# Dilated and sliding-window attention with a GEGLU block: batch 1's dilated q, k turned by DMA, and values of late dilated pairs laid side by side again

## The chip, the cores and the metric

The kernel runs on one core of a Trainium2 chip. The metric is device time in microseconds, from several executions of each kernel; a smaller number is better. A profile of one execution comes with each kernel. TensorE is called PE in the profile, VectorE DVE, ScalarE ACT, GpSimd POOL and SyncE SP; a "q" behind a name means its queue, where transfers are issued.

## The reference

Attention runs over 8 batches of 8 heads, 576 tokens, 64 values a head. Heads 0 to 3 look back over a window of 32 tokens ("plain"), heads 4 to 7 over every fourth token of 128 ("dilated"). The result, 4608 rows of 512, goes through a gated layer of 1536 hidden values.

```python
mask_plain = (rel >= 0) & (rel < window)                                        # window 32
mask_dil = (rel >= 0) & (rel < window * dilation) & (rel % dilation == 0)       # dilation 4
scores = np.where(masks[None, :, :, :], scale * np.matmul(q, k.transpose(0, 1, 3, 2)), -1000000000.0)
attn = np.exp(scores - np.max(scores, axis=-1, keepdims=True))
attn = attn / (np.sum(attn, axis=-1, keepdims=True) + 1e-09)
x = np.matmul(attn, v)                       # then (batch, token) x (head, value) = 4608 x 512
# ...
g = x @ w_gate                               # 512 x 1536
gelu = 0.5 * g * (1.0 + erf(g * inv_sqrt2))
return (gelu * (x @ w_val) @ w_out).astype(np.float32)
```

## The kernel before

The work is ordered by hand; each engine runs its instructions in the order in which the program emits them. Heads are taken two at a time, so there are 32 "pairs": pairs 4b to 4b+3 belong to batch b. Two of each batch are plain and two dilated (in batches 2 and 3 the dilated ones come first). A pair has scores (`emit_s`: matmuls, then the exponential on ScalarE into a tile `P`, then the mask on VectorE), and values (`emit_pv` or `emit_both`: matmuls for the numerator and the denominator, then the division on VectorE into `xT`).

The gated layer is taken in 9 stages `c` of 512 tokens. A stage has a hidden layer (`ffn1`, 12 blocks of 8 matmuls; gelu on ScalarE, product on VectorE into `u_all`), then an output layer (`ffn2`, 4 blocks of 12 matmuls, one bank each). Scores and values of later pairs are set between these matmuls: `scores[c]` lists the pairs whose scores are made in stage c, `values_b[c]` those whose values are made in its output layer, `values_a[c]` those in its hidden layer (key: the block). `places` says after which matmul of which output block: v values, s scores, m mask, x division.

How batch 1 gets its turned dilated q and k (rows of eight tokens, 72 rows; 32 turns on TensorE through `ident`, then four copies out of PSUM):

```python
    def t_dil(b, hp, q8, b0, engs):
        qtd_ = tiles["qT", b][1]
        for t in range(2):
            for hl in range(2):
                for r in range(4):
                    c0 = ((hl * 2 + r % 2) * 2 + r // 2) * R8
                    nc.tensor.transpose(ps16[:, b0 + t, c0 : c0 + R8],
                        q8[:, t, 2 * hp + hl, 2 * r : 2 * r + 2, :].rearrange("p r d -> p (r d)"),
                        ident[0:R8, 0:R8])
            copy(engs[t], qtd_[...], ps16[...])          # cut

    # ... loads of batch 1
    sv1 = new_v(1)
    new_qt(1)
    qd1 = load_eights(1)
    wo1 = [load_wo(i) for i in range(3)][1]
    load_v_dil(1)
    q61 = ldp.tile([R6, 2, 6, HK, D], F16, tag="qp", name="qp1")
    for hp in range(2):
        for t in range(2):
            cast_six("pool", q61, st1, t, hp)
    gate["dma"] = wo1            # the next load on SyncE waits for this one to land
    v_plain(1, sv1, nc.sync)
    v_cast(1, sv1)
    tiles["plain", 2] = load_batch_plain(2)
```

Batches 2 to 7 are turned by DMA:

```python
    def load_batch_rest(b):
        # ...
        dst = qtd_.rearrange("p t h m i -> p (t h m) i")
        nc.sync.dma_start_transpose(out=dst[:, :, 0:P], in_=qd.rearrange("p t h r d -> p (t h r d)"))
        nc.sync.dma_start_transpose(out=dst[:, :, P:NCL], in_=rd.rearrange("p t h r d -> p (t h r d)"))
        # ...
        last_keys(b, 0, HK, nc.gpsimd)       # copies the last 64 keys of each class into kTr
```

Stage 0's output layer (pairs 4 and 5 are batch 1's plain ones, 6 and 7 its dilated ones; `third(tb, i)` is four output matmuls):

```python
            s_of(4)
            t_dil(1, 0, qd1, 0, ("dve", "dve"))
            t_dil(1, 1, qd1, 2, ("act", "dve"))
            mask_next()
            last_keys(1, 0, HK)
            third(0, 0)
            s_of(5)
            third(1, 0)
            mask_next()
            den(4, 0)
            s_of(6)
            third(0, 1)
            # ... cut
```

Values in the hidden layers, in one pass over v and ones: the tile of v holds v of one head, ones, v of the other head, so that 128 columns of it give a numerator and its denominator together. Dilated pairs do so in batches 5 to 7 only (`spread`):

```python
    def emit_both(n, b0):
        # ... plain pairs cut
                for s in range(2):
                    o = ps[:, b0 + 2 * hl + s, 0:DW].rearrange("p (m i) -> p m i", m=2)
                    src = pt[:, 2 * s + hl, :].rearrange("p (m i) -> p m i", m=2)
                    for m in range(2):
                        mm(o[:, m, 0:P], vd[:, hp, 2 * m + s], src[:, m, 0:P], hl, m == 0)
                    mm(o[:, :, P:NCL], vr[:, hp, s], src[:, :, P:NCL], hl, False)
```

Its division is two transposes of 64 rows (L537), a reciprocal, a transpose and two products of 64 rows (L550). `emit_pv` instead makes denominators by a matmul with ones and numerators by one with v, each for 64 output rows, and its division has one transpose (L576) and one product (L602) of 128 rows.

Of the kernel before, what the change touches and what calls it, by code (L numbers as in the profile page):

```python
# [9 lines left out]
F16 = mybir.dt.float16  # L10
# [11 lines left out]
def kernel(  # L22
# [14 lines left out]
    P = 128  # L37
# [22 lines left out]
    prb = ctx.enter_context(tc.tile_pool(name="prb", bufs=7))  # L60
# [17 lines left out]

# [4 lines left out]
            const.tile([P, HP, 4, 3, D], F16, tag=f"vd{i}", name=f"vd{i}"),  # L83
            const.tile([P, HP, 3, D], F16, tag=f"vt{i}", name=f"vt{i}"),
            const.tile([P, HP, 2, 3, D], F16, tag=f"vr{i}", name=f"vr{i}"),
# [65 lines left out]


    values_a = {3: {4: 16}, 4: {1: 20, 4: 21, 8: 22}, 5: {1: 24, 4: 25, 8: 26}, 6: {1: 28, 4: 29, 7: 30, 10: 31}}
    all_at = [n for at in values_a.values() for n in at.values()]
    spread = (5, 6, 7)

# [37 lines left out]
    def new_v(b):  # L194

        sv = ldp.tile([P, 5, HK, D], F32, tag="sv", name=f"sv{b}")
        tiles["v", b] = vset[b % 3]
        if b in spread and b - 3 not in spread:
            for t in vset[b % 3][1::2]:
                nc.gpsimd.memset(t.rearrange("p g r x d -> p (g r) x d")[:, :, 1, :], 1.0)  # L200
        return sv

    def side_by_side(t):

        n = HK * t.shape[2] * D
        flat = t.rearrange("p g r x d -> p (g r x d)")[:, 0:n]
        return flat.rearrange("p (h r d) -> p h r d", h=HK, d=D)

    def v_dil(b, h, s0, rest=False):

        t = tiles["v", b][3 if rest else 1]
        return t[:, h // 2, s0, 2 * (h % 2), :] if b in spread else side_by_side(t)[:, h, s0, :]
# [49 lines left out]
    def load_v(b, dst, src):  # L262

        if b not in spread:
            nc.gpsimd.dma_start(out=fl(side_by_side(dst)), in_=src)
            return
        for h in range(HK):
            nc.gpsimd.dma_start(  # L268
                out=dst[:, h // 2, :, 2 * (h % 2), :], in_=src[:, h, :].rearrange("p (r d) -> p r d", d=D)
            )  # L270

    def load_v_dil(b):
        load_v(b, tiles["v", b][1], quads(v, b, HK, 0, 4 * P))
        load_v_dil_rest(b)

    def load_v_dil_rest(b):
        for m in range(2):
            src = quads(v, b, HK, S - 256, S)[:, :, 2 * m * D : 2 * m * D + 2 * D]
            load_v(b, tiles["v", b][3][64 * m : 64 * m + 64], src)
# [11 lines left out]
    def load_batch_rest(b):  # L291
# [6 lines left out]
        qtp_, qtd_, _ = tiles["qT", b]  # L298
        dst = qtd_.rearrange("p t h m i -> p (t h m) i")
        nc.sync.dma_start_transpose(out=dst[:, :, 0:P], in_=qd.rearrange("p t h r d -> p (t h r d)"))  # L300
        nc.sync.dma_start_transpose(out=dst[:, :, P:NCL], in_=rd.rearrange("p t h r d -> p (t h r d)"))
        dst = qtp_.rearrange("p t h c -> p (t h) c")
# [14 lines left out]

    def in_one(n):

        return n in all_at and (is_plain(n) or n // NHP in spread)  # L320
# [108 lines left out]
    def emit_pv(n, b0, parts=("den", "num"), wide=False, flip=False):  # L429
# [4 lines left out]
        vp, _, vt, _ = tiles["v", b]  # L434
# [39 lines left out]
        else:  # L474
# [10 lines left out]
            if "num" in parts:  # L485
                for s in range(2):
                    for m in range(3):
                        for hl in range(2):
                            h, p0 = 2 * hp + hl, (2 * s + hl) * DW
                            if m < 2:  # L490
                                lhs, c0 = v_dil(b, h, 2 * m + s), 512 * (s + flip) + m * NCL
                                add(hl, c0, run(P), lhs, p0 + m * NCL, run(P), m == 0)
                            else:
                                two = [[NCL, 2], [1, 16]]
                                add(hl, 512 * (s + flip) + P, two, v_dil(b, h, s, True), p0 + P, two, False)
# [3 lines left out]
    def emit_both(n, b0):  # L499

        b, hp = n // NHP, n % 2
        pt = tiles["P", n]
        vp, vd, vt, vr = tiles["v", b]

        def mm(o, trio, rhs, hl, st):
            lhs = trio[:, hl : hl + 2, :].rearrange("p x d -> p (x d)")
            nc.tensor.matmul(o, lhs, rhs, start=st, stop=True, skip_group_check=True)  # L509

        for hl in range(2):
            if is_plain(n):
                for j in range(5):
                    w = (PW, PW, PW, P, PT)[j]
                    p0 = j * PW - (32 if j == 4 else 0)
                    o = ps[:, b0 + 2 * hl + j // 4, j % 4 * P : j % 4 * P + w]
                    mm(o, vp[:, j, hp] if j < 4 else vt[:, hp], pt[:, hl, p0 : p0 + w], hl, j in (0, 4))
            else:
                for s in range(2):
                    o = ps[:, b0 + 2 * hl + s, 0:DW].rearrange("p (m i) -> p m i", m=2)  # L520
                    src = pt[:, 2 * s + hl, :].rearrange("p (m i) -> p m i", m=2)
                    for m in range(2):
                        mm(o[:, m, 0:P], vd[:, hp, 2 * m + s], src[:, m, 0:P], hl, m == 0)
                    mm(o[:, :, P:NCL], vr[:, hp, s], src[:, :, P:NCL], hl, False)
# [4 lines left out]
    def norm_both_r(n, b0):  # L529
        dt = nrm.tile([P, 18, 32], F32, tag="dt", bufs=1)  # L530
        for hl in range(2):
            dst = dt[64 * hl : 64 * hl + 64].rearrange("p b c -> p (b c)")
            if is_plain(n):
                nc.vector.transpose(dst, both_rows(1 - hl, b0, hl))  # L534
            else:
                src = ps[64 - 64 * hl : 128 - 64 * hl, b0 + 2 * hl : b0 + 2 * hl + 2, 0:DW]
                nc.vector.transpose(dst.rearrange("p (s c) -> p s c", s=2), src)  # L537
# [440 lines left out]
```

The softmax here doesn't subtract the row's maximum and nothing guards it: scores larger than these inputs give would overflow.

## Time and profile before

| what | value |
|---|---|
| device time, median of 3 | 350.09 us (349.64 to 350.47) |
| span of the profiled run | 348.4 us |
| busy share PE / DVE / ACT / POOL | 97% / 60% / 43% / 29% |
| matmuls of the hidden layer (L627), 864 | 227.8 us busy |
| matmuls of the output layer (L661), 420 | 97.0 us busy |
| PE 20 to 43 us (hidden layer of stage 0), DMA | 211 GB/s |
| PE 43 to 62 us (output layer of stage 0) | 18.65 of 19.00 us busy |

In a line of the timeline the columns are start, duration, engine, line of the kernel, operation, tiles out<-in, shape and count; in brackets stands how long the engine was idle before, and what ended it. Busy times of PE overlap, as matmuls are pipelined, so the distance of starts tells more than their durations. In the list of waits the columns are total, count and longest wait. In the chain they are start, duration and what ran.

### The profile page before, as it was taken

To read this page: it belongs to the slowest core of one execution; us is meant where nothing else is said; L and a number is where in the kernel's file an instruction comes from. 1 tells how busy PE (TensorE), PEld (TensorE's weight loads), DVE (VectorE), ACT (ScalarE), POOL (GpSimd) and SP (SyncE) were. 2 spreads that over 40 slices of the span, in tenths; PEclk is the share of its full clock that TensorE was granted. 3 is DMA by queue.
4 is the path that set the end of the run, shared out by engine and by line. 5 is a ranking of instruction groups with operands and counts; after the bars stand their busy time and mean duration, and the time that the engine had idled before them with its cause. 6 is when DMAs were issued, how large, how long until landed. Compare 5 with 4: busy or idle time off the path is not lost.

```text
span 348.4 us, 6007 instructions
## 1 busy us (share of the span) xinstructions
PE 336.6 (97%) x2322; PEld 163.9 (47%) x2322; DVE 210.2 (60%) x317; ACT 148.1 (43%) x220; POOL 102.0 (29%) x154
## 2 busy tenths in 40 slices
PE   8979999999999999999999999999999999999996
PEld 3644454444544445444544444445444444444443
DVE  4884497533784379664989865996399723303320
ACT  2753372535543546336553456326532223323321
POOL 8693304630630560493009800670000000000000
PEclk9999999999999999999999999999999999999999
DMA  8999999999999999796169944991100020020002
GB/s 184 225 206 222 203 203 174 178 143 257 180 121 251 190 126 227 168 167 115 61 158 179 121 96 131 205 120 48 74 2 0 32 90 1 2 87 33 0 33 90
DMA packets 113037, 44.45 MB, mean 128 GB/s; under 512 B 91408, under 2 KB 108432, under 8 KB 113008
## 3 DMA queue, kind: packets, MB, share of 16 engines
q1 hardware_dynamic: 84192, 31.01, 38.4%
q0 software_dynamic: 28272, 12.33, 30.5%
q10 hardware_dynamic: 544, 0.72, 0.7%
q8 instruction: 18, 0.29, 0.3%
q14 instruction: 11, 0.09, 0.1%
HBM read 39.85 MB, written 9.44 MB: 141 GB/s over the span
## 4 chain that ended last, share of the span: by engine, by line
PE 71%; DVE 11%; DMA 10%; issue 3%; ACT 3%; SPq 1%; POOL 1%; DVEq 0%; POOLq 0%; ACTq 0%
PE ps L627 41%; PE ps L661 22%; DMA st<-in_k_dram 4%; PE ps L497 3%; DMA sv<-in_v_dram 3%; DMA wv<-in_moe_w_val_dram 3%; DVE u_all L650 2%; DVE dt L537 1%; DVE dt L576 1%; DVE xT L550 1%; PE ps L509 1%; PE ps L415 1%; DVE rb L587 1%; DVE P L425 1%; DVE xT L602 1%
## 5 line engine op out<-in xcount | busy, mean ns | idle before, releaser
L649 ACT ACTIVATE g<-ps 128x512 f16<-128x512 f32 x108 | 63.9, 597 | 124.4 <-PE ps L627 123.9
L650 DVE SCALAR_TENSOR_TENSOR u_all<-g,ps 128x512 f16<-128x512 f16 x108 | 72.5, 683 | 73.4 <-PE ps L627 63.1
L627 PE MATMUL ps<-xT,wv 128*128 128x512 f16 x432 | 113.8, 379 | 1.1 <-DMA wv<-in_moe_w_val_dram 0.6
L627 PE MATMUL ps<-xT,wg 128*128 128x512 f16 x432 | 114.0, 379 | 0.7 <-POOL xT L750 0.4
L661 PE MATMUL ps<-wo,u_all 128*128 128x512 f16 x420 | 97.0, 380 | 0.3 <-DVE qTd L328 0.2
L627 PEld LDWEIGHTS <-wv 128*128 128x128 f16 x432 | 42.2, 98 | 53.7 <-issue 2.6
L627 PEld LDWEIGHTS <-wg 128*128 128x128 f16 x432 | 41.2, 98 | 48.1 <-issue 0.8
L661 PEld LDWEIGHTS <-u_all 128*128 128x128 f16 x420 | 38.4, 98 | 45.0 <-issue 0.8
L241 POOL CAST qp<-st 128x2048 f16<-128x2048 f32 x6 | 11.4, 1894 | 94.1 <-DMA st<-in_k_dram 72.9
L672 ACT ACTIVATE osb<-ps 128x512 f32<-128x512 f32 x33 | 19.7, 597 | 39.8 <-PE ps L661 39.8
L587 DVE STREAM_TRANSPOSE rb<-rc 128x576 f32<-128x576 f32 (+4 forms) x34 | 25.3, 743 | 1.3
L417 ACT ACTIVATE P<-ps 128x1152 f16<-128x1152 f32 x16 | 18.1, 1131 | 10.9 <-PE ps L415 10.7
L395 ACT ACTIVATE P<-ps 128x960 f16<-128x960 f32 x16 | 15.5, 971 | 9.8 <-PE ps L385 9.8
L576 DVE STREAM_TRANSPOSE dt<-ps 128x576 f32<-128x576 f32 x17 | 13.2, 778 | 9.5 <-PE ps L497 9.3
L425 DVE TENSOR_TENSOR P<-P,mask_d 128x1152 f16<-128x1152 f16 x13 | 10.3, 789 | 10.3 <-ACT P L417 10.3
L602 DVE TENSOR_TENSOR xT<-ps,rb 128x576 f16<-128x576 f32 x12 | 13.4, 1134 | 2.2 <-PE ps L497 1.9
L268 POOL DMA_DIRECT2D vr<-in_v_dram x24 | 14.1, 596 | 1.5 <-DMA vd<-in_v_dram 1.4
L425 DVE TENSOR_TENSOR P<-P,mask_p 128x1344 f16<-128x1344 f16 x14 | 11.8, 854 | 4.3 <-ACT P L396 4.3
L225 POOL CAST vp<-sv 128x1024 f16<-128x1024 f32 x8 | 8.4, 1055 | 12.3 <-DMA sv<-in_v_dram 12.3
L534 DVE STREAM_TRANSPOSE dt<-ps 64x576 f32<-64x576 f32 x14 | 10.9, 781 | 0.4
L674 DVE TENSOR_SCALAR osb<-ps 128x512 f32<-128x512 f32 x2 | 1.4, 692 | 15.7 <-PE ps L661 15.7
L497 PE MATMUL ps<-P,ones 128*64 128x96 f16 (+5 forms) x154 | 9.6, 241 | 1.1 <-DVE P L425 0.8
(96 smaller groups left out, 279.4 us busy)
## 6 DMA issues: line engine op xcount, KB each, us to landing
out_dram<-osb SPq DMA_DIRECT2D x35, 256.0 KB, 2.0
sv<-in_v_dram SPq DMA_DIRECT2D x40, 128.0 KB, 3.0
st<-in_q_dram SPq DMA_DIRECT2D x24, 128.0 KB, 4.0
st<-in_k_dram SPq DMA_DIRECT2D x24, 128.0 KB, 2.9
wg<-in_moe_w_gate_dram POOLq DMA_DIRECT2D x3, 512.0 KB, 7.4
wv<-in_moe_w_val_dram POOLq DMA_DIRECT2D x3, 512.0 KB, 9.7
wo<-in_moe_w_out_dram POOLq DMA_DIRECT2D x3, 512.0 KB, 20.0
qd<-in_q_dram POOLq DMA_DIRECT2D x6, 256.0 KB, 5.2
```

What stands on the lines that cost most here:

```text
L395: nc.scalar.activation(pt[:, :, 0:PB], sb[:, 0, :, 0:PB], AF.Exp, bias=0.0, scale=scale)
L417: nc.scalar.activation(pt, ps[:, b0 : b0 + 4, 0:DW], AF.Exp, bias=0.0, scale=scale)
L425: nc.vector.tensor_tensor(pt, pt, mb, ALU.mult)
L497: nc.tensor.matmul(o, lhs, rhs, start=st, stop=True, skip_group_check=True)
L576: nc.vector.transpose(dst, den)
L587: nc.vector.transpose(rb[:, 0 : 32 * nb].rearrange("p (b c) -> p b c", c=32), bass.AP(tensor=rc.tensor, offset=rc.offset, ap=[rc.ap[0], [1 ...
L602: nc.vector.tensor_tensor(dst.rearrange("p (i m s) -> p i m s", m=2, s=2), num, rb.rearrange("p (s m i) -> p i m s", s=2, m=2), ALU.mult,)
L627: nc.tensor.matmul(ps[:, bank, :], w[:, kc, ns], xT[kc][:, tok], start=first, stop=end)
L649: nc.scalar.activation(g, ps[:, banks[0], :], AF.Gelu)
L650: nc.vector.scalar_tensor_tensor(u_all[:, nb, :], g, USCALE, ps[:, banks[1], :], ALU.mult, ALU.mult)
L661: nc.tensor.matmul(ps[:, bank, :], u_all[:, fc, tb * P : (tb + 1) * P], wo_t[fc // 4][:, fc % 4, :], start=(fc == 0), stop=(fc == NNB - 1),)
L672: nc.scalar.activation(osb, ps[:, bank, :], AF.Copy, bias=0.0, scale=1.0 / USCALE)
```

## The change

Two things are exchanged. In the place of the 32 turns of batch 1's dilated q and k stand two transposing transfers, as in the later batches; for this q and k come as rows of four tokens (qd, and rd for the last 16 rows). The output layer of stage 0 begins with output blocks between the scores, so that the turned q and k are asked for later. And the values of dilated pairs in batches 5 to 7 are no longer made in one pass: v lies side by side without ones, and these pairs use `emit_pv` as the other dilated ones do. With this the scores and values of stages 3 to 6 are spread anew, and there is one more buffer for P.

```diff
-    prb = ctx.enter_context(tc.tile_pool(name="prb", bufs=7))
+    prb = ctx.enter_context(tc.tile_pool(name="prb", bufs=8))
...
-            const.tile([P, HP, 4, 3, D], F16, tag=f"vd{i}", name=f"vd{i}"),
+            const.tile([P, HK, 4, D], F16, tag=f"vd{i}", name=f"vd{i}"),
...
+    def turn_dil(b, qd, rd):
+        dst = tiles["qT", b][1].rearrange("p t h m i -> p (t h m) i")
+        nc.sync.dma_start_transpose(out=dst[:, :, 0:P], in_=qd.rearrange("p t h r d -> p (t h r d)"))
+        nc.sync.dma_start_transpose(out=dst[:, :, P:NCL], in_=rd.rearrange("p t h r d -> p (t h r d)"))
...
-    qd1 = load_eights(1)
+    qd1, rd1 = load_qk_dil(1)
     wo1 = [load_wo(i) for i in range(3)][1]
     load_v_dil(1)
...
     gate["dma"] = wo1
     v_plain(1, sv1, nc.sync)
+    turn_dil(1, qd1, rd1)
     v_cast(1, sv1)
...
-    scores = {1: range(8, 12), 2: range(12, 17), 3: range(17, 23), 4: range(23, 28), 5: range(28, 32)}
-    values_b = {1: range(8, 12), 2: range(12, 16), 3: range(17, 20), 4: range(23, 24), 5: range(27, 28)}
-    values_a = {3: {4: 16}, 4: {1: 20, 4: 21, 8: 22}, 5: {1: 24, 4: 25, 8: 26}, 6: {1: 28, 4: 29, 7: 30, 10: 31}}
+    scores = {1: range(8, 12), 2: range(12, 17), 3: range(17, 22), 4: range(22, 27), 5: range(27, 32)}
+    values_b = {1: range(8, 12), 2: range(12, 16), 3: range(17, 20), 4: range(22, 24), 5: range(27, 28)}
+    values_a = {3: {4: 16}, 4: {2: 20, 6: 21}, 5: {1: 24, 4: 25, 7: 26}, 6: {1: 28, 4: 29, 7: 30, 10: 31}}
...
-        3: "0.0m 0.6s 0.6m 1.5v 1.5s 1.5x 1.5m 2.4v 2.4s 2.4x 2.4m 2.11s 2.11m 3.6v 3.6s 3.6x 3.6m",
-        4: "0.0m 1.3v 1.3s 1.3x 1.3m 2.1s 2.1m 2.10s 2.10m 3.6s 3.6m",
-        5: "0.0m 1.3v 1.3s 1.3x 1.3m 2.3s 2.3m 3.1s 3.1m",
+        3: "0.0m 1.3v 1.3s 1.3x 1.3m 2.5v 2.5s 2.5x 2.5m 2.11s 2.11m 3.4s 3.6v 3.6x 3.6m",
+        4: "0.0m 1.3v 1.3s 1.3x 1.3m 2.4v 2.4s 2.4x 2.4m 2.11s 2.11m 3.7s 3.7m",
+        5: "0.0m 1.3v 1.3s 1.3x 1.3m 2.1s 2.1m 2.10s 2.10m 3.6s 3.6m",
...
-                (norm_both_x if in_one(pend) else norm_x)(pend, SB)
+                (norm_both_x if is_plain(pend) else norm_x)(pend, SB)
...
             s_of(4)
-            t_dil(1, 0, qd1, 0, ("dve", "dve"))
-            t_dil(1, 1, qd1, 2, ("act", "dve"))
+            third(0, 0)
+            third(1, 0)
+            mask_next()
+            s_of(5)
+            third(0, 1)
+            den(4, 0)
+            third(1, 1)
             mask_next()
             last_keys(1, 0, HK)
-            third(0, 0)
-            s_of(5)
-            third(1, 0)
+            s_of(6)
+            third(0, 2)
+            den(5, 0)
             mask_next()
-            den(4, 0)
-            s_of(6)
-            third(0, 1)
+            third(1, 2)
+            s_of(7)
+            den(6, 0)
             mask_next()
-            third(1, 1)
-            den(5, 0)
-            s_of(7)
-            third(0, 2)
-            mask_next()
-            den(6, 0)
-            third(1, 2)
-            ffn2(c, 2, 0, {3: [lambda: num(4, 4)], 8: [lambda: den(7, 0)]})
+            ffn2(c, 2, 0, {5: [lambda: num(4, 4)], 9: [lambda: den(7, 0)]})
```

The order of the output layers of stages 1 and 2 changes by one place at most, and the helpers of the old layout of v go.

## The prediction

> **What bounds the kernel now.** I read the page first (engines, chain), then TensorE's timeline stage by stage, then the queue of SyncE. The chain belongs to TensorE:
>
> ```profile
> PE 71%; DVE 11%; DMA 10%; issue 3%; ACT 3%; SPq 1%; POOL 1%; DVEq 0%; POOLq 0%; ACTq 0%
> ...
> L649 ACT ACTIVATE g<-ps 128x512 f16<-128x512 f32 x108 | 63.9, 597 | 124.4 <-PE ps L627 123.9
> ```
>
> The second line shows ScalarE idle for 123.9 us waiting for matmuls, so the other engines are slack. A stage's hidden work is cheap; only what stops TensorE counts. 96 matmuls of the hidden layer take 20.8 us in the chain, 0.217 us each. Two places with stops matter here: stage 0's output and the last dilated pairs. First TensorE in stage 0's output:
>
> ```profile
> 43.51 0.47 PE L385 MATMUL ps<-qTp 64*128 64x160 f16 x10
> 43.91 1.50 PE L357 MATMUL ps<-ident,qd 72*128 72x72 f16 x32
> 45.66 1.02 PE L661 MATMUL ps<-wo,u_all 128*128 128x512 f16 x4 [0.25 <-DVE qTd L328]
> 46.61 0.55 PE L385 MATMUL ps<-qTp 64*128 64x160 f16 x10
> ```
>
> The 32 turns (L357) hold 43.91 to 45.66: 1.75 us. Scores of pair 6, the first reader of batch 1's dilated q and k, start at 48.48; the stage ends at 61.39. Now SyncE's queue in the same time, then the one row on it from its list of waits:
>
> ```profile
> 45.46 4.44 SPq L217 DMA_DIRECT2D sv<-in_v_dram  x5
> ...
> 57.18 6.09 SPq L217 DMA_DIRECT2D sv<-in_v_dram  x5
> 63.38 2.75 SPq L300 DMA_TRANSPOSE qTd<-qd  x1
> 66.25 1.15 SPq L301 DMA_TRANSPOSE qTd<-rd  x1
> ```
> ```profile
> SPq L217 <- DMA wo<-in_moe_w_out_dram: 17.4, 1, 17.4
> ```
>
> The row at 45.46 is batch 1's v: it stood 17.4 us behind the second block of w_out, which is its gate. The two transposes of batch 2 occupy the queue 2.75 and 1.15 us; what they cost to landing is in GpSimd's timeline:
>
> ```profile
> 72.42 0.62 POOL L289 COPY kTr<-qTd 128x512 f16<-128x512 f16 x1 [3.33 <-DMA qTd<-rd]
> ```
>
> The copy of the last keys waited for the second transpose until 72.4, some 9 us after the first was issued at 63.38.
>
> **What the skill says.** "DMA: Bandwidth & Descriptors", section "DMA Transpose (X-bar)": the plain DMA transpose is issued from Sync or Scalar only; here all stand in SyncE's queue, as the trace shows. The same page, "Issuing engines are not separate DMA queues": transfers of all queues share the same 16 engines. The trace agrees: between 20 and 43 us they move 211 GB/s at a busy share over 1, weights and batch 1's q, k together. "TensorE: Matmul & The Clock Gate", section "What's actually happening": after an idle window of about 3.4 us the array falls to half clock until it has been busy as long. The first warm-up matmuls here stand 0.43 us apart until 6.2 us, later ones 0.217; no idle stretch of 3.4 us inside this run shows the fall.
>
> **The change, part by part.**
>
> *Removed in stage 0:* 32 turns and four copies, 1.75 us of TensorE. As they come just before the wait below, this is not gained.
>
> *Added:* two small loads (rd) and two transposes. In the built program SyncE's order is: batch 1's five loads of v (behind the gate, still the second block of w_out), then transpose qd, transpose rd, then batch 2's loads. So:
> 1. The gate opens at 45.46 before. Its queue on GpSimd carries the same bytes ahead of it (2 x 288 KB of q, k before; 2 x 256 + 2 x 32 after), in smaller pieces, and two more issues of 0.53. I take 46.0.
> 2. Five loads of v: 4.43 us, to 50.4.
> 3. From the issue of the first transpose to the landing of the second: 9.0 us for batch 2, beside other loads. For an emptier queue I estimate 8.0 from the row's own figures: 2.75 + 1.15 of issue, and about 4 more (landing of the second 4.8 to 7.4 us after its issue). Landing at 58.4.
> 4. The copy of the last keys, now on VectorE, 0.29, and a hand-over: scores of pair 6 at 58.8.
>
> By then TensorE has done what lies ahead: scores of 4 and 5, 16 output matmuls, one denominator. The loads of GpSimd move this too. A load there waits for the landing of the eighth before it (vr stood 1.5 and 3.5 us for wg and wv at 29 and 33 us); with two loads more, both vr of batch 1 come to wait for qd (landing 14.4 to 16.9 us after issue, so 37.6 and 40.8). The four casts behind them then begin about 41.5 instead of 35.5 and 40.0, and the plain turns, at 40.3 and 42.9 now, slip about 2.3 us. Even so TensorE runs dry near 52. It waits some 7 us.
>
> After pair 6 there remain 32 output matmuls (6.9 us), two scores, three denominators, four numerators. VectorE orders mask 6 after denominator 5's transpose, reciprocal, transpose (0.78 + 0.27 + 0.78, about 2 with gaps), so denominator 6 starts about 4.6 after pair 6; by the same sums the stage ends about 12.7 after pair 6. Before it ended 12.9 after (61.39 - 48.48). So the delay passes through whole: 58.8 - 48.5 = +10.3. If 7 us of idling halve the clock for the next 3.5 to 4 us, some 1.5 more, since one wait of 1.4 (on mask 6) absorbs part. Stage 0: **+11.8**.
>
> *Values of pairs 22, 26, 30, 31 (v side by side again):* one pass of 12 matmuls over 128 output rows (262.91 to 263.51, 0.60 us) becomes 4 + 12 matmuls over 64 rows that run two at a time: in stage 0 the same shapes take 0.37 and half of 0.68, so 0.7. Four pairs: +0.4 on TensorE. On VectorE a pair had 2 x 0.78 + 0.27 + 0.78 + 2 x 1.12 = 4.85 us and gets 0.78 + 0.27 + 0.78 + 1.13 = 2.96. That matters, as these chains stop TensorE:
>
> ```profile
> 267.73 1.11 DVE xT L550
> 268.84 0.03 issue
> 268.87 1.14 DVE xT L550
> 270.01 0.04 issue
> 270.05 0.42 PE ps L509 x6
> ...
> 273.98 0.66 DVE u_all L650
> 274.63 0.04 issue
> 274.68 1.47 PE ps L661 x6
> ```
>
> Pair 31 cannot write its banks until pair 30's product has read them, and the output layer waits for the last u. From the starts of successive matmuls I count stops of 0.18 + 0.90 + 0.26 in stage 6, 0.66 at the end of stages 4 and 5 each (scores wait for L550), 0.29 + 0.43 and 0.17 earlier in them. Shorter chains and pair 22's move into the output stage should take about 2.6 of these 3.5.
>
> *Scores spread 4,5,5,5,5 instead of 4,5,6,5,4:* stage 3 drops the second score at its sixth block, which stopped TensorE 0.82 (159.53 to 160.59, on the exponential behind its table load). New score and value hooks in 4 and 5 may stop it 0.2 to 0.3 each, as 201.95 and 238.79 do now (0.20). Gain 0.3. The eighth P buffer lets scores run ahead and costs no time.
>
> Later stages: +0.4 - 2.6 - 0.3, with 0.4 for a changed mixture of scores and blocks also gained in stages 4 and 5: **-2.9**. GpSimd loses 36 issues of 0.6 to 0.75, none on the path. Batch 2's loads are held by about 4 us by SyncE's order, but its first scores are needed at 82 us before, now 94. Sum: 350.1 + 11.8 - 2.9 = 359.0; the clock penalty being unsure, I say 358.3.
>
> **Rivals.**
> - *The transposes land in time.* Then 1.75 us go from stage 0 and 2.9 later: 345.5. For it: the new order, with output blocks set ahead of pair 6, looks made to cover a late arrival, and a transpose takes only about 9 us. Against it: they cannot be issued before the gate, about 46, and the blocks end near 52.
> - *The stop comes earlier and smaller.* SyncE's fifth load of v stood long in the queue (the five took 4.43 here, 2.76 for batch 3); with 2.8 for the five and a gate at 45.4 pair 6 starts at 56.6: +8.1, less clock loss, and 355 to 356.5.
> - *The late landing spreads into batch 2.* Its loads wait for completion slots held by the two transposes; if stage 1's last scores were reached first, 1 to 3 more: 360 to 362. Against: about 12 us of slack in the landing of batch 2's turned q, k (77.5 against 91 when plain ones are read).
> - *The 64-row value passes hurt.* At 0.4 us in all they cannot weigh.
>
> **Range and chances.** The stop in stage 0 is 8 to 13 us with clock, the later gain 1.5 to 4: 353.5 to 362 holds it 8 times in 10. Slower by 2% begins at 357.1, just under my middle, so slower 0.6. Within 2% takes the smaller stop and the case with none: 0.37. Faster by 2% needs 343.1, beyond even the first rival: 0.03.
>
> **What would show it.** Right: pair 6's scores at 56 to 60 us instead of 48.5, with idle time of 5 to 8 us put down to the copy kTr or to the transposed load; transposes on SyncE's queue issued at about 50; matmuls of 0.43 spacing after the stop; no stop over 0.4 us at the end of stages 4 to 6. Wrong: transposes issued before 46, or landed within 4 us of issue; a stage 0 that ends before 63; stops on VectorE in the hidden layers of stages 4 to 6 as long as now.

## The result and the profile after

The changed kernel takes 355.94 us (median of 4, 355.73 to 356.49) against 350.26 for the kernel before on the same chip (4 executions): ratio 1.0167, 95% interval 1.0149 to 1.0186. It is slower by 5.7 us, but by less than 2%. The span of the profiled execution is 353.8 us (before 348.4), so the two traces differ by 5.4.

The chain of the page, and below it the costliest group of ScalarE:

```profile
PE 69%; DVE 12%; DMA 9%; issue 3%; POOL 3%; SPq 3%; ACT 1%; DVEq 0%; POOLq 0%; ACTq 0%
...
L600 ACT ACTIVATE g<-ps 128x512 f16<-128x512 f32 x108 | 64.0, 596 | 123.4 <-PE ps L578 122.7
```

TensorE still carries the chain and ScalarE still waits 122.7 us for it. New is SyncE's queue (SPq), up from 1% to 3%: transfers and their issue have got onto the path. In this kernel L612 is a matmul of the output layer, L578 of the hidden layer, L354 and L384 scores of plain and dilated pairs, L466 values, L394 a mask, L265 the copy of the last keys.

The chain in order of time, cut to 43 to 70 us (start, duration, what ran), shows where:

```profile
26.73 16.66 DMA wo<-in_moe_w_out_dram
...
43.41 0.39 SPq L196
...
51.54 2.57 DMA qTd<-rd
...
54.13 0.31 DVE kTr L265
...
54.48 0.45 PE ps L384 x8
```

Read downwards: the second block of w_out lands at 43.4, five loads of v are issued (L196 and four more like it), then the transposes, the second of which lands at 54.10; the keys are copied; pair 6 gets its scores. In the kernel before, the same stretch of the chain has only TensorE in it. TensorE's own timeline there:

```profile
48.69 1.04 PE L612 MATMUL ps<-wo,u_all 128*128 128x512 f16 x4
53.78 0.39 PE L384 MATMUL ps<-qTd 64*128 64x128 f16 x4 [4.05 <-DMA qTd<-qd]
54.48 0.21 PE L384 MATMUL ps<-qTd,kTr 64*128 64x32 f16 x2 [0.31 <-DVE kTr L265]
...
54.86 1.89 PE L612 MATMUL ps<-wo,u_all 128*128 128x512 f16 x4
...
57.39 1.89 PE L612 MATMUL ps<-wo,u_all 128*128 128x512 f16 x4
```

After 4.05 us of waiting, four output matmuls take 1.89 us where the same four took 1.04 at 48.69: the array runs at half clock until about 59 (the granted clock is halved from 52.4 to 59.2). SyncE's queue, and below it its row of waits for w_out:

```profile
43.41 4.71 SPq L196 DMA_DIRECT2D sv<-in_v_dram  x5
48.23 3.20 SPq L254 DMA_TRANSPOSE qTd<-qd  x1
51.54 1.15 SPq L255 DMA_TRANSPOSE qTd<-rd  x1
```
```profile
SPq L196 <- DMA wo<-in_moe_w_out_dram: 15.3, 1, 15.3
```

The gate stood 15.3 us, not 17.4, and opened at 43.4, not 45.5. Batch 2's copy of keys on GpSimd, later by some 3 us than before, is still long before batch 2's scores:

```profile
75.77 0.61 POOL L265 COPY kTr<-qTd 128x512 f16<-128x512 f16 x1 [5.21 <-DMA qTd<-rd]
```

By stage, from the first matmul of each layer to the first of the next, in us:

| stage and layer | before | after | difference |
|---|---|---|---|
| 0 hidden (with the turns of batch 1) | 25.21 | 23.60 | -1.61 |
| 0 output | 15.74 | 23.94 | +8.20 |
| 2 output | 16.02 | 16.35 | +0.33 |
| 3 output | 15.76 | 14.90 | -0.86 |
| 4 hidden, output | 24.30, 13.08 | 22.61, 14.41 | -1.69, +1.33 |
| 5 hidden, output | 23.77, 12.58 | 23.31, 13.09 | -0.46, +0.51 |
| 6 hidden, output | 24.12, 10.63 | 23.59, 10.36 | -0.53, -0.27 |
| 8 output (to the end of the span) | 13.73 | 14.09 | +0.36 |

The others agree within 0.03. Stage 0's output layer ends at 68.06 us instead of 61.39, +6.67 (the stage begins 0.09 later); all that follows is 1.23 shorter; the sum is the 5.4 between the spans.

The waits of TensorE from 174 to 282 us (stages 4 to 6), before and then after, show what the shorter chains of division took away:

```profile
PE ps L509 <- DVE xT L550: 0.7, 1, 0.7
PE ps L415 <- DVE xT L550: 0.5, 1, 0.5
PE ps L385 <- DVE xT L550: 0.5, 1, 0.5
PE ps L627 <- DVE u_all L650: 0.3, 1, 0.3
```
```profile
PE ps L466 <- DVE P L394: 0.6, 1, 0.6
```

All four waits on the product (L550) and on u_all are gone; one new wait for a mask has come, in stage 4's output layer.

### The profile page after: what moved, and what is told of

It is laid out like the page before. It is cut to its first block, busy times and chain, and to the rows that moved or that the text cites. A ratio compares the mean times of both kernels' runs of the same rounds, so it can differ in the third digit from the quotient of the medians.

```text
span 353.8 us, 5942 instructions
## 1 busy us (share of the span) xinstructions
PE 337.0 (95%) x2310; PEld 162.5 (46%) x2310; DVE 200.9 (57%) x306; ACT 147.6 (42%) x219; POOL 83.7 (24%) x123
## 4 chain that ended last, share of the span: by engine, by line
PE 69%; DVE 12%; DMA 9%; issue 3%; POOL 3%; SPq 3%; ACT 1%; DVEq 0%; POOLq 0%; ACTq 0%
PE ps L578 41%; PE ps L612 21%; DMA wo<-in_moe_w_out_dram 5%; PE ps L466 4%; DMA sv<-in_v_dram 3%; SPq L196 2%; DVE dt L494 2%; DVE u_all L601 2%; DVE rb L538 2%; DVE dt L527 2%; DVE xT L553 1%; DVE xT L504 1%; DVE P L394 1%; PE ps L384 1%; PE ps L354 1%
## 5 line engine op out<-in xcount | busy, mean ns | idle before, releaser
L600 ACT ACTIVATE g<-ps 128x512 f16<-128x512 f32 x108 | 64.0, 596 | 123.4 <-PE ps L578 122.7
L578 PE MATMUL ps<-xT,wg 128*128 128x512 f16 x432 | 114.0, 379 | 0.8 <-POOL xT L701 0.4
L578 PE MATMUL ps<-xT,wv 128*128 128x512 f16 x432 | 113.8, 379 | 0.7 <-DMA wv<-in_moe_w_val_dram 0.5
L612 PE MATMUL ps<-wo,u_all 128*128 128x512 f16 x420 | 99.1, 385 | 0.0
L578 PEld LDWEIGHTS <-wv 128*128 128x128 f16 x432 | 42.2, 98 | 53.0 <-issue 1.8
L578 PEld LDWEIGHTS <-wg 128*128 128x128 f16 x432 | 41.3, 98 | 48.7 <-issue 1.1
L612 PEld LDWEIGHTS <-u_all 128*128 128x128 f16 x420 | 38.5, 98 | 44.7 <-issue 1.6
L527 DVE STREAM_TRANSPOSE dt<-ps 128x576 f32<-128x576 f32 x21 | 16.4, 779 | 17.7 <-PE ps L466 17.6
L553 DVE TENSOR_TENSOR xT<-ps,rb 128x576 f16<-128x576 f32 x16 | 17.9, 1131 | 2.0 <-PE ps L466 1.7
L394 DVE TENSOR_TENSOR P<-P,mask_d 128x1152 f16<-128x1152 f16 x13 | 9.7, 748 | 9.7 <-ACT P L386 9.7
L394 DVE TENSOR_TENSOR P<-P,mask_p 128x1344 f16<-128x1344 f16 x14 | 12.3, 892 | 4.0 <-ACT P L365 4.0
L466 PE MATMUL ps<-P,ones 128*64 128x96 f16 (+5 forms) x174 | 11.5, 249 | 2.6 <-DVE P L394 1.9
L466 PEld LDWEIGHTS <-ones 128*64 128x64 f16 x174 | 7.2, 110 | 12.2 <-issue 9.9
L265 POOL COPY kTr<-qTd 128x512 f16<-128x512 f16 (+1 forms) x7 | 4.1, 583 | 29.9 <-DMA qTd<-rd 24.2
```

Source lines behind the costliest of these rows:

```text
L394: nc.vector.tensor_tensor(pt, pt, mb, ALU.mult)
L527: nc.vector.transpose(dst, den)
L553: nc.vector.tensor_tensor(dst.rearrange("p (i m s) -> p i m s", m=2, s=2), num, rb.rearrange("p (s m i) -> p i m s", s=2, m=2), ALU.mult,)
L578: nc.tensor.matmul(ps[:, bank, :], w[:, kc, ns], xT[kc][:, tok], start=first, stop=end)
L600: nc.scalar.activation(g, ps[:, banks[0], :], AF.Gelu)
L612: nc.tensor.matmul(ps[:, bank, :], u_all[:, fc, tb * P : (tb + 1) * P], wo_t[fc // 4][:, fc % 4, :], start=(fc == 0), stop=(fc == NNB - 1),)
```

## The experiments

Every run is compared with runs of the kernel before on the same chip (350.25 to 350.59 us there).

### Are the two halves of the change independent?

The late half alone: stage 0 as before, all else as changed.

```diff
-    qd1, rd1 = load_qk_dil(1)
+    qd1 = load_eights(1)
...
-    turn_dil(1, qd1, rd1)
...  (stage 0's output layer as in the kernel before)
```

> The changed kernel with stage 0 as it was before (32 turns on TensorE, q and k of batch 1 as rows of eight, the old order of its output layer); only the later stages are changed. By the stage lengths of the two traces the later stages gain 1.3: 349.0 (348.6 to 349.4). By my prediction they gain 2.9: 347.4. If the two parts work on each other (a later stage shortened only because stage 0 was long) it is 350.3.

Measured: 349.16 us (348.94 to 349.32), ratio 0.9950 (0.9935 to 0.9965). Stages 2 to 7 differ from before as in the table above, and from the end of stage 0 on this run is 1.61 us shorter than the kernel before. The +0.36 of stage 8 is absent here. It goes with the two transposes: the seven runs that have them take 14.08 or 14.09 us from the first output matmul of stage 8 to the end, the six without them 13.70 to 13.73, and among these is the run below that differs from the changed kernel only in leaving them out (13.72). In the traces SyncE ends with a row of waits for transfers, taken in a fixed order. Without the transposes the last store's wait stands last, and the span ends 0.92 to 0.93 us after that store's landing. With them six more waits of 0.06 us follow it, and the end comes after 1.29 to 1.30. So the turn costs +6.67 in stage 0 and +0.36 at the end.

The turn alone: the kernel before with the new stage 0.

> The kernel before with stage 0 as changed (two transposes behind the gate, the new order), the later stages and the layout of v as before. The sum of stage 0's two stretches in the traces says +6.7: 356.9 (356.3 to 357.5). If late loads of batch 2 reach into later stages it is more, 358 and above.

Measured: 357.63 us (357.15 to 357.92), ratio 1.0191 (1.0172 to 1.0210). This is just above the range given. Stage 0's output is +8.20, as in the whole change, and the halves add up: +7.04 and -1.43 make +5.61, the whole change +5.68. In the profiled execution two later stages, untouched by the edit, lost 0.72 and 0.22. The first of these is in stage 1's output layer; VectorE's timeline and GpSimd's there:

```profile
91.10 2.06 DVE L430 TENSOR_TENSOR P<-P,mask_d 128x1152 f16<-128x1152 f16 x1 [1.45 <-ACT P L422]
```
```profile
90.66 1.90 POOL L241 CAST qp<-st 128x2048 f16<-128x2048 f32 x1 [12.52 <-DMA sv<-in_v_dram]
```

A mask (median 0.76 us in the kernel before) took 2.06 beside a GpSimd cast of 1.90 us. In the whole change the same mask ends before that cast begins (93.44), takes 0.76, and neither stage loses anything. "SBUF — State Buffer", section "Who interferes with whom", says that a VectorE instruction with two inputs in SBUF contends with a GpSimd instruction that reads SBUF, and that the loser waits for the whole of the other. The numbers agree roughly: the cast ends at 92.56, 1.46 after the mask began, and 1.46 + 0.76 is 2.22, not far from 2.06.

### What did the idle time do to the clock?

Nineteen matmuls of ones are set into the wait, so that TensorE isn't idle while it waits for the turned q.

```diff
             last_keys(1, 0, HK)
+            warm(19, 4)
             s_of(6)
```

> The changed kernel with 19 matmuls of 128x512 that nobody reads set ahead of pair 6's scores, where TensorE waits 4.2 us; they take about 4.1 us and add nothing if the wait stays. Theory (idling halves the clock, and the matmuls after it stand 0.42 us apart until 58.6): the output layer of stage 0 after pair 6 takes 12.7 us instead of 14.3, 354.4 us in all (354.0 to 354.9). Rival (the wide spacing comes from the waits on VectorE and transfers, not from the clock): 355.9 to 356.3.

Measured: 354.50 us (354.23 to 354.77), ratio 1.0103 (1.0086 to 1.0120). TensorE's timeline, then busy times and granted clock (the column after POOL's) for stage 0's output, of this run and then of the changed kernel:

```profile
49.74 4.26 PE L652 MATMUL ps<-ones 128*128 128x512 f16 x19
...
54.53 0.19 PE L384 MATMUL ps<-qTd,kTr 64*128 64x32 f16 x2 [0.31 <-DVE kTr L265]
...
54.79 1.04 PE L612 MATMUL ps<-wo,u_all 128*128 128x512 f16 x4
```
```profile
44.10:66.60 22.50, 20.16 (x169) 9.17 (x165) 13.62 (x21) 8.44 (x12) 6.03 (x7) 1.00 1.10 181
```
```profile
44.13:68.07 23.94, 18.40 (x151) 7.82 (x147) 13.49 (x22) 8.59 (x12) 7.49 (x10) 0.86 1.11 187
```

Pair 6 begins 0.16 later than in the changed kernel and the layer is yet 1.4 us shorter, the output matmuls again 1.04 for four. So of the 6.67 us lost in stage 0, 1.4 are the clock. The other 5.3 are the wait together with what the new order costs by itself, which the next runs take apart.

### What would the order have cost with nothing to wait for?

The two transposes are left out and their target is filled with a constant by VectorE long before; order and all other work stay. Batch 1's dilated pairs are then computed from constants, so this is a time without the turn, not a kernel.

```diff
     v_plain(1, sv1, nc.sync)
-    turn_dil(1, qd1, rd1)
+    nc.vector.memset(tiles["qT", 1][1].rearrange("p t h m i -> p (t h m i)"), 0.01)
```

> The changed kernel without the turning of batch 1's dilated q and k: the two transposes are left out and VectorE fills their target with a constant early on; everything else, the loads and the order too, stays. It shows the new order when nothing is waited for. Theory: pair 6's scores then wait for the copy of the last keys, which stands on VectorE behind pair 4's transposes and mask 5; they start at 51 to 52, and the output layer of stage 0 ends at 64 to 65, still 3 later than before: 352.0 (351.2 to 353.0). Rival (my first rival: all of the stop is the transposes' landing, and 1.75 us of turns are gained): the stage ends at 59 to 60, 347 to 348.

Measured: 353.23 us (352.50 to 353.75), ratio 1.0077 (1.0060 to 1.0093). That is at the upper end of the range given and a little beyond; the clock fell in three of its four executions (granted 0.995) but not in the profiled one (352.50 us). Even without a transfer to wait for, the new stage 0 ends at 65.3, 3.9 later than before (0.2 of it because the stage begins later). TensorE, VectorE and GpSimd in their timelines:

```profile
50.10 0.29 PE L384 MATMUL ps<-qTd 64*128 64x128 f16 x4
53.00 0.19 PE L384 MATMUL ps<-qTd,kTr 64*128 64x32 f16 x2 [2.62 <-DVE kTr L265]
...
57.33 0.44 PE L466 MATMUL ps<-P,ones 128*64 128x288 f16 x4 [1.29 <-DVE P L394]
```
```profile
51.13 1.41 DVE L394 TENSOR_TENSOR P<-P,mask_p 128x1344 f16<-128x1344 f16 x1
52.46 0.48 DVE L265 COPY kTr<-qTd 128x512 f16<-128x512 f16 x1
```
```profile
50.79 1.04 POOL L204 CAST vp<-sv 128x1024 f16<-128x1024 f32 x1 [7.75 <-DMA sv<-in_v_dram]
```

The copy of the keys stands on VectorE behind pair 4's two transposes and mask 5, and mask 5 in turn ran 1.41 instead of 0.86 beside GpSimd's cast. Pair 6 waits 2.62 us for a copy of 0.48, and denominator 6 waits 1.29 for its mask. The order is itself a cost that the late transfer covers.

The same without the turn, but in the old order moved up by one place: keys copied right behind mask 4, masks ahead of the denominators.

```diff
             mask_next()
+            last_keys(1, 0, HK)
             s_of(5)
             third(0, 1)
-            den(4, 0)
-            third(1, 1)
             mask_next()
-            last_keys(1, 0, HK)
+            den(4, 0)
             s_of(6)
...
```

> As the run without the turning, with the keys copied right after mask 4 and the scores of pairs 6 and 7 as early as in the kernel before, but two blocks of output matmuls ahead of pair 5's scores. Theory (the stage is bound by exponential, mask and denominator of one pair after another; removing the 32 turns gains only what of their 1.75 us was not hidden in the wait for pair 4's exponential): the stage ends at 60 to 61.4, 348.0 (347.6 to 349.2). Rival (the turns' 1.75 us come back in full): 346.8 to 347.3.

Measured: 349.15 us (348.94 to 349.62), ratio 0.9964 (0.9950 to 0.9977), the time of the late half alone. Stage 0 ends at 61.88, before 61.39 (it begins 0.30 later here). Busy times in two stretches of equal length, this run from its first output matmul and the kernel before from its first turn, each to the end of the layer (the second number of a row is PE busy):

```profile
44.40:61.88 17.48, 15.91 (x151) 7.56 (x147) 12.27 (x21) 8.59 (x12) 4.70 (x7) 1.00 1.16 197
```
```profile
43.91:61.39 17.48, 17.13 (x182) 8.56 (x178) 14.57 (x25) 9.11 (x13) 3.87 (x6) 1.00 1.14 190
```

TensorE has 1.2 us less to do and takes as long. What holds it instead, in this run's timeline:

```profile
46.82 0.23 PE L354 MATMUL ps<-qTp 64*128 64x160 f16 x1 [0.52 <-ACT P L364]
47.20 0.45 PE L354 MATMUL ps<-qTp 64*128 64x160 f16 x9 [0.15 <-ACT P L365]
...
50.65 0.48 PE L466 MATMUL ps<-P,ones 128*64 128x512 f16 x6 [0.20 <-DVE dt L527]
...
53.17 0.44 PE L466 MATMUL ps<-P,ones 128*64 128x288 f16 x4 [0.70 <-DVE dt L527]
```

Pair 5's scores wait for pair 4's exponential; they begin at 46.6 before, 46.6 after and 46.8 here. The 32 turns had lain in that wait, for nothing: 1.57 us of stops have taken the place of the 1.75. A perfect DMA turn, at no cost at all, was worth nothing in this order.

### What decides when the turned q, k land?

My theory after the result was the order on SyncE's queue: the transposes stand behind five loads of v, which stand behind the gate. The rival: what else is on the 16 transfer engines. So the turn was issued ahead of the gate.

```diff
+    turn_dil(1, qd1, rd1)
     gate["dma"] = wo1
     v_plain(1, sv1, nc.sync)
-    turn_dil(1, qd1, rd1)
```

> The changed kernel, with the two transposes of batch 1 issued ahead of the gated loads of v instead of behind them; nothing else differs. Theory (the place in SyncE's queue, behind the gate, makes the stop): they are issued at about 39 us, when q and k have landed, and have landed by 46; the matmuls of pair 6 no longer wait for a transfer but for the copy of the last keys, which stands on VectorE behind the chain of pair 4 and mask 5, so they start at 51.5 to 52 instead of 53.8 to 54.5; idle time of TensorE there about 2 us, no half clock after it, the output layer of stage 0 ends near 64.5 instead of 68.1, 352.3 us in all (351.5 to 353.2). Rival one (all of the wait is the transfer's): stage 0 ends near 60, 347 to 348. Rival two (a transpose takes as long as the traffic beside it, wherever it is issued): 355 to 356.

Measured: 354.04 us (351.95 to 356.56, 10 executions, widely spread), ratio 1.0093 (1.0067 to 1.0120). SyncE's queue, and the landing times of all transposes into the tile qTd:

```profile
38.34 6.37 SPq L254 DMA_TRANSPOSE qTd<-qd  x1
```
```profile
DMA to landing us min/median/max: 4.9/7.7/12.8
```

Issued 9.9 us earlier, the first lands at 51.15 (12.8 after issue, the longest of all), only 2.6 earlier than in the changed kernel, the second at 52.97, only 1.1 earlier. Its issue took 6.37 us instead of 3.20. Pair 6 waits 1.76 us for the transfer and 1.93 for the copy of the keys, and stage 0 ends at 66.50, not near 64.5. My theory fell for the larger part. The spread goes with the clock: the three executions with a granted clock of 1.0 took 351.95 to 352.89 us, the seven others (0.989 to 0.995) 353.84 to 356.56.

Earlier still: batch 1's dilated q, k are loaded ahead of the third weights, and the turn is issued when they land (with the better order of stage 0, and the later place of pair 22's values from the next section).

> The change mended: batch 1's dilated q and k loaded ahead of the third weights of the hidden layer, both transposes issued ahead of the gated loads, the order of the run before this one, and the later value hook. Theory (a transpose lands late because weights stand in front of it at the same 16 engines; issued near 32 it lands before 46): no stop at pair 6, 347.3 if the weights still come in time, up to 349 if the third weights, 3 us later than now, stop the hidden layer of stage 0 at its ninth block (34 us). Rival (transposes land late wherever they are issued while weights are loading): landing at 50 to 53, 351 and above.

Measured: 352.24 us (351.48 to 353.23), ratio 1.0050 (1.0032 to 1.0068). SyncE's queue, the landing times, and TensorE:

```profile
29.42 11.73 SPq L254 DMA_TRANSPOSE qTd<-qd  x1
```
```profile
DMA to landing us min/median/max: 4.5/7.1/21.9
```
```profile
38.44 1.04 PE L578 MATMUL ps<-xT,wv 128*128 128x512 f16 x4 [1.88 <-DMA wv<-in_moe_w_val_dram]
```

Issued 18.8 us earlier than in the changed kernel, it lands at 51.3, within 0.2 of the run before. Pair 6 still waits 0.71 and 0.51 us, so the rival was right. And the weights, now behind q and k, came late and stopped the hidden layer for 1.88 us. Whether issued at 29.4, 38.3 or 48.2, the first transpose lands at 51.3, 51.2 and 53.7. These times have a pattern: of the loads issued ahead of it, on whichever queue, the last to land did so at 48.45, 49.70 and 51.61, and the transpose 2.9, 1.5 and 2.1 us later. In the run at 29.4 that load is the third block of w_out, issued just before it at 28.3.

Then the traffic was cleared away: the turn is issued early, and the third block of w_out and batch 1's v wait until it has landed.

```diff
-    wo1 = [load_wo(i) for i in range(3)][1]
-    load_v_dil(1)
+    for i in range(2):
+        load_wo(i)
...
+    turned = turn_dil(1, qd1, rd1)
+    gate["dma"] = turned
+    gated(load_wo(2))
+    load_v_dil(1)
-    gate["dma"] = wo1
+    gate["dma"] = turned
     v_plain(1, sv1, nc.sync)
-    turn_dil(1, qd1, rd1)
```

> The changed kernel with the two transposes issued as soon as batch 1's q, k have landed, and with the third block of w_out, batch 1's dilated v and plain v made to wait until the second transpose has landed; ahead of the transposes only two blocks of w_out remain. Theory (what stands on the transfer engines ahead of or beside the transposes sets their landing): issued near 38.3 us as with the early turn, but landed near 45 to 47 instead of 51.2 and 53.0; TensorE then waits only as it does in the changed order with nothing to turn, pair 6's scores near 50, and the time is about 353.2, ratio 1.008. Rival (a transpose issued in this stretch is slow by itself, or is held to a fixed point near 51): landing at 50 to 53 again, pair 6's scores at 51 or later, time 354 or more.

Measured: 355.62 us (354.69 to 356.69), ratio 1.0155 (1.0132 to 1.0178). SyncE's queue, the landing times, and TensorE:

```profile
38.94 5.16 SPq L254 DMA_TRANSPOSE qTd<-qd  x1
44.22 1.15 SPq L255 DMA_TRANSPOSE qTd<-rd  x1
```
```profile
DMA to landing us min/median/max: 3.1/7.3/9.3
```
```profile
51.73 0.19 PE L384 MATMUL ps<-qTd,kTr 64*128 64x32 f16 x2 [1.82 <-DVE kTr L265]
...
54.35 1.87 PE L612 MATMUL ps<-wo,u_all 128*128 128x512 f16 x4 [2.30 <-DMA wo<-in_moe_w_out_dram]
```

The landing came to 46.96 and 47.29 (3.1 after the second's issue, the shortest), as the traffic theory says: the last load issued ahead of the first transpose, the second block of w_out, landed at 44.22, 2.7 us before it. A transpose isn't slow by itself. But the time is no better: the held-back block of w_out lands at 54.3 and stops TensorE 2.30 us, and the clock halves all the same (1.87 for four matmuls). I had expected 353.2 and not thought of the third block. The copy of the keys behind mask 5 stops TensorE here too (1.82).

The same loads in the better order:

> The same loads, with the older, shifted order of stage 0's output (the last keys copied behind mask 4, masks of 5 and 6 ahead of their denominators) and the later place for pair 22's values. Theory: with landing near 46 no wait for the turned q, k is left; stage 0's output takes about 18.7 us as in the run of this order without turns, and the time is 348.4 to 349.2, as without the turn by DMA at all: nothing gained by the transposes, nothing lost. Rival: landing near 51 stops TensorE as in the run with loads first, 351 to 352.5.

Measured: 353.18 us (352.74 to 354.29), ratio 1.0078 (1.0058 to 1.0098); a fourth execution took 690.87 us and is left out. TensorE:

```profile
53.13 1.02 PE L612 MATMUL ps<-wo,u_all 128*128 128x512 f16 x4 [2.46 <-DMA wo<-in_moe_w_out_dram]
...
58.66 0.55 PE L466 MATMUL ps<-P,vp 128*64 128x160 f16 x8 [2.52 <-POOL vp L204]
```

Pair 6 no longer waits at all, and TensorE stops for w_out and then for batch 1's v instead (2.46 and 2.52). My expectation, 348.4 to 349.2, was wrong by the same omission. But this doesn't show that there is more to bring than the engines can bring in time. Busy times around the gate (the last two columns are the share and the GB/s of the transfer engines):

```profile
44.00:45.00 1.00, 1.00 (x6) 0.49 (x5) 0.59 (x1) 0.99 (x2) 0.00 (x0) 1.00 1.45 280
45.00:48.00 3.00, 2.32 (x22) 0.98 (x20) 1.06 (x2) 2.48 (x4) 0.79 (x2) 1.00 0.11 21
```

While the loads stand behind their gate the engines are all but idle: 21 GB/s for three microseconds (10 GB/s from 46 to 48 us in the run before this one). At the 200 GB/s of the stretches around it I estimate that this pause alone would have carried the third block of w_out, 512 KB. So the holding back made these loads late at least in part. No run issues the third block of w_out right behind the transposes without a gate, so whether all could land in time stays open. In the kernel before none of these transfers stops TensorE.

### Stages 2 and 4

Stage 4's output layer grew by 1.33, in it the new wait for a mask (first section). There pair 22's values have a division of 2.96 us on VectorE, and pair 23's mask stands behind it. From the late half alone, these values were moved to the eighth matmul of their block and the next scores to the last block.

```diff
-        4: "0.0m 1.3v 1.3s 1.3x 1.3m 2.4v 2.4s 2.4x 2.4m 2.11s 2.11m 3.7s 3.7m",
+        4: "0.0m 1.3v 1.3s 1.3x 1.3m 2.8v 2.8s 2.8x 2.8m 3.1s 3.1m 3.7s 3.7m",
```

> As the run with the later stages alone (stage 0 as before, 349.2 us), with the second value hook of stage 4's output layer four matmuls later (after matmul 8 instead of 4 of its third block; the scores behind it move to the next free places). Theory (the output layer of stage 4 is 1.3 longer than before because pair 23's values wait 0.78 for their mask, which stands on VectorE behind pair 22's division): that stop goes, 348.4 (348.1 to 348.7). Rival (the added pair costs its matmuls and the stop only moves to another hook): 349.0 to 349.4.

Measured: 348.40 us (348.04 to 348.47), ratio 0.9938 (0.9925 to 0.9950). The time is as expected, but only partly for the reason given. The layer has +1.01 instead of +1.33: the wait for the mask no longer stands in the list of waits, yet only 0.3 us came back. The rest of the difference to the run with the late half alone lies in stage 0's start and hidden layer (0.6 in the two traces), which the edit doesn't touch.

And pair 16's score back to its old place in stage 2:

```diff
-        2: "0.0m 1.3v 1.3s 1.3x 1.3m 2.5v 2.5s 2.5x 2.5m 3.0s 3.0m 3.6v 3.6x 3.7s 3.12w 3.12m",
+        2: "0.0m 1.3v 1.3s 1.3x 1.3m 2.5v 2.5s 2.5x 2.5m 3.0s 3.0m 3.6v 3.6s 3.6x 3.12w 3.12m",
```

> Late changes alone with the later place for pair 22's values, and with pair 16's score back where the kernel before has it in stage 2 (after the sixth matmul of the last block, ahead of the division). Theory (the moved score is what costs stage 2's output 0.33 us, as its exponential ends too late for the denominators): stage 2's output is back at 16.02 us, and the time is 348.0 to 348.3, ratio 0.993. Rival (the 0.33 comes from the eighth P buffer or the changed order of pools, not from this place): stage 2's output stays at 16.35 and the time at 348.4.

Measured: 347.97 us (347.77 to 348.56), ratio 0.9932 (0.9916 to 0.9948). TensorE at the end of stage 2, of the changed kernel and then of this run:

```profile
142.31 0.49 PE L466 MATMUL ps<-P,ones 128*64 128x64 f16 x10 [0.25 <-ACT P L365]
```
```profile
135.25 0.49 PE L466 MATMUL ps<-P,ones 128*64 128x64 f16 x10
```

The wait for the exponential is gone and the layer takes 16.05 us, as before: one matmul of the output layer later, and behind the division, was the whole 0.33. This version, the late half with two places mended and the 32 turns left on TensorE, is faster than the kernel before and the changed one.

## Why the prediction was right, and where not

The time fell into the range (353.5 to 362), 2.4 us under the middle of 358.3, in part by luck: stage 0 was put 5.1 us too high and the later gain 1.7 too high, and the two errors cancel in part. What was predicted did run as described: transposes behind the gate and v, TensorE dry, half clock, delay passed through. But as a cause the late landing is only part of it. With nothing to turn, the new order loses 3.9 of the 6.67 us by itself, as the copy of the keys stands behind mask 5 on VectorE (2.62 us of waiting). Step 4 counted 0.29 and a hand-over for that copy and no cost of the order. The landing itself adds some 2.8, about half of it by the clock.

**The gate (step 1).** Taken at 46.0, measured 43.4. I argued from smaller pieces and two more issues. In the changed kernel and in the one with the turn alone, batch 1's qd lands 13.8 to 14.5 us after issue, in the kernels with rows of eight 14.4 to 17.4, though the bytes are as many. Which of two differences does it isn't settled: the form of the rows, or that rd's two completion slots hold the loads of v behind them back (vd is issued at 33.0 instead of 26.9). No run has one without the other. For the form of the rows speaks the run with the cleared queue: there the third block of w_out and all of batch 1's v were issued only after 47 us, and qd landed 13.8 and 14.4 us after issue all the same.

**The loads of v (step 2)** took 4.71 for 4.43. **The transposes (step 3)** took 5.9 us from first issue to second landing, not 8.0. These three give -2.6, +0.3 and -2.1, so the second landed at 54.1 instead of 58.4. That figure was drawn from batch 2's transposes, which ran among other loads; the runs showed that what is issued ahead decides: the first transpose landed 5.5 us after its issue here, and after 8.0, 12.8 and 21.9 in the runs that issued it earlier.

**Pair 6 and the rest of the stage (step 4).** 58.8 became 53.78. The remaining 12.7 and 1.5 for the clock, 14.2 together, came to 14.28; the 1.5, given as unsure, is 1.4 in the run that fills the wait. So the +11.8 became +6.7, the 5.0 of pair 6's start and hardly anything else. TensorE ran dry at 49.7, not near 52, and "waits some 7 us" was 4.05 and 0.31. In the prediction I said that no idle stretch inside the run showed the fall of the clock, which "TensorE: Matmul & The Clock Gate", section "What's actually happening", gives for idle windows of about 3.4 us. Now one does, but the traces need less than that: the clock fell 2.6 us into this wait, in the run with the cleared queue after waits of 1.82 and 2.30 us, in the next run after one of 2.52, while waits of 2.46 there and of 2.62 with nothing to turn passed without a fall. Half clock then lasted 6.83, 6.83 and 3.41 us.

**GpSimd's loads.** That both vr would wait for qd was right (3.72 and 0.79 us), but as qd came sooner, the four casts began at 39.47 instead of 41.5, and TensorE's plain turns, at 40.3 before, began at 40.40 and did not slip by 2.3.

**Turns removed: "not gained".** Right, but for a second reason than the one given. I named the wait just behind them; the run without any turn shows that pair 4's exponential would have kept the 1.75 us anyway.

**Later stages.** -2.9 expected, -1.23 measured, or -1.6 without the 0.36 at the end, which the two transposes bring and the prediction didn't have. The stops in the hidden layers went as expected; -1.69, -0.46 and -0.53 there and -0.86 in stage 3. Part of this is only work that moved and comes back elsewhere: a score (0.4 of TensorE, as from 140.40 to 140.80 in the changed kernel) from stage 3 to stage 5, where the +0.51 stands, and pair 22's values (about 0.65) from stage 4's hidden to its output layer. What failed: I put no price on the new places. Pair 22's values in the output layer brought the wait for mask 23 (0.6), and the moved score 0.33 in stage 2. The "0.4 for a changed mixture of scores and blocks" showed nowhere. A pass over 64 rows cost less than said: 269.10 to 269.74, 0.64 us against 0.60.

**The rivals.** "The stop comes earlier and smaller", 355 to 356.5, is what happened: gate and loads together were ahead of my first choice by 2.3 us. But it put pair 6 at 56.6, for it kept the 8.0 of step 3, and its time fits only because it kept the -2.9 too. "The transposes land in time", 345.5, is refuted twice over: they didn't, and with nothing to turn this order would be at 353.2, because of the copy of keys behind mask 5 and a denominator's wait for its mask. Batch 2 didn't come into it: its stages 1 and 2 are unchanged but for the 0.33.

**Signs named.** Half clock spacing and issue at about 50 (48.2) came; pair 6 "at 56 to 60" didn't; no stop above 0.4 us is left in the hidden layers of stages 4 to 6.

## What to carry to other kernels

Before moving work from a busy engine to a transfer, look at what that engine does next: 32 turns that filled a wait that was there anyway were free, and their replacement had to be free as well to break even. Don't expect an earlier issue to bring data earlier by as much: 10 and 19 us earlier brought 2.6 and 2.4 us here. Look at what has been issued ahead, on every queue, and when it lands. Holding other loads back brought the landing forward by 6.8 us, but left the engines idle, and the held loads then stopped TensorE. And when an order is built to cover a late arrival, price it with the arrival taken away: here it alone cost 3.9 us.

## What I had not expected of the hardware

- The issue of one and the same transpose occupied SyncE's queue for 3.20 us (at 48.2), 6.37 (at 38.3) or 11.73 (at 29.4), and the second transpose stood behind it: 41.27 in the last case.
- The same transpose landed at 51.2 to 51.3 us from issues 9 us apart, and at 46.96 when w_out's third block and v were held back. "DMA: Bandwidth & Descriptors", section "Queues, rings and completion order", says that each engine takes turns between its queues by packets, and that a completion is written only after the engine's earlier writes of all queues. Either could hold a transpose back; no run here tells them apart.
- A mask beside a GpSimd cast: 2.06 us for 0.76, 1.41 for 0.86. There the cast had begun first. With nothing to turn and the better order a mask began first (51.71) and took 0.71; the cast (51.76) took 0.93 instead of 0.40.
- Two transfers more in stage 0 cost 0.36 us at the very end, in SyncE's closing row of waits.
